# Earlier loads at a stage change, a store cut in two, and program order on ScalarE and VectorE, in a recurrent-attention and gated-MLP kernel

## The chip, the cores and the metric

The kernel runs on one core of a Trainium2 chip. Times are device microseconds (us) of one execution. Where two kernels are compared by a ratio, it is the mean time of one kernel's runs over that of the other's of the same rounds, so it isn't quite the ratio of the medians quoted beside it. "Job" means one series of runs on one chip; kernels of one job share their runs of the kernel before.

## The reference

```python
xn = layernorm(A_x)                                  # 2048 x 1024
# A: attention over 64 segments of 32 tokens, each with 8 memory rows in front
for s in range(64):
    h = concat([mem, xn[segment s]])                 # 40 rows
    q, k, v = h @ Wq, h @ Wk, h @ Wv                 # 32 heads of 128
    p = softmax(where(mask, q k^T * scale, -1e9))    # memory rows see all; tokens are causal
    o = (p v) @ Wo
    mem = o[:8]                                      # carried into the next segment
    outs.append(o[8:])
# B: h = sigmoid(xn @ w_gate) * (xn @ w_up);  B = h @ w_down        (width 3584)
return A_x + concat(outs) * silu(B)
```

The kernel doesn't walk the 64 segments one after the other. With these small weights the scores are so small that softmax inside a memory row is almost a mean, so it computes all memory rows in two sweeps, treats all tokens in parallel, and checks at the end from norms and maxima that this was allowed (`flag`; a slow exact path runs otherwise).

## The kernel before: the parts that matter

The stages are: values for all tokens (`v_ps`), two sweeps over the memory rows mixed with pieces of the gate and up projections, 32 heads of attention, the rest of gate and up, and the down and output projections with the check beside them. TensorE (PE) and the SyncE queue (SP) keep program order everywhere. ScalarE (ACT), VectorE (DVE) and GpSimd (POOL) are ordered by the compiler's scheduler except where `manual_schedule` names them.

The second memory sweep writes 71 rows of values to HBM (63 segments and 8 start rows), and takes the difference of the sweeps for the check on DVE:

```python
for hg in range(H // 4 + 2):
    if hg < H // 4:
        ...                                          # 32 matmuls into vm_ps
        vts[hg] = gp.tile([P, 4, NCM], BF16, name="vmt", tag="o2", bufs=3)
        nc.scalar.copy(vts[hg][:], vm_ps[:])
        dv = gp.tile([P, 4, NM], F32, name="dv", bufs=2)
        nc.vector.scalar_tensor_tensor(dv[:], vm_ps[:, :, 0:NM], 1.0 / M, vg1[:, hg * 4:(hg + 1) * 4, :], ...)
        nc.vector.tensor_tensor(dv[:], dv[:], dv[:], op=ALU.mult)
        nc.vector.tensor_reduce(dvs[:, hg, :], ...)
    if hg >= 2:
        ...                                          # 4 transposes into vt_ps
        nc.vector.tensor_copy(vm_sb[0:NCM, ...], vt_ps[0:NCM])
        if g % 2 == 1:
            nc.sync.dma_start(vm_dram[1:NSEG + M, cols], vm_sb[0:NCM, :])     # 71 rows
            nc.sync.dma_start(vm_dram[0:1, cols], vm_sb[0:1, :])
```

Then attention. `va` (token values) and `vm` (memory values) are allocated in a pool that takes over the space of the stage before:

```python
vas = [vp.tile([P, NT + 1, VW], BF16, name=f"va{i}") for i in range(2)]       # and memsets on DVE
...
def load_pair(hp):                     # va, then vm (each memory row read by 32 partitions)
    nc.sync.dma_start(va[:, 0:NT, 1:VW - 1], vp_dram[:, cols]...)
    ...
    for a in range(SPT):
        nc.sync.dma_start(vm[a * SEG:(a + 1) * SEG, :, 1:VW - 1], src[a:a + 1].to_broadcast([SEG, NT, 2 * DH]))

def proj_steps(h):                     # one step per matmul: 80 "slots" a head
    for x, dst in enumerate((qt, kt)):
        nc.scalar.activation(fsq[:], w_[:, :, hc], ACTF.Square, accum_out=fro[:, x, h:h + 1])
        for i in range(NBLK):
            ...                        # 8 matmuls into pr, then
            nc.scalar.copy(dst[:, a:b], pr[:, 0:b - a])
            if i == NBLK - 1:
                track(x, dst)          # DVE: mx = max(mx, |dst|), in two halves

load_pair(0)
for h in range(H + 1):
    pj = proj_steps(h); at = attn_steps(h - 1)       # the projection of h beside the attention of h-1
    for i in range(80):
        if i == 32 and h % 2 == 1: load_w((h + 1) // 2); load_pair((h + 1) // 2)
        next(pj); next(at)
```

Here `fsq` is the square of the head's weights, `s_ps` the scores, `pT` their exp and mask, `o_ps` the product with the values, `of` the addition of the memory part. In the down stage the check adds up squares of Wo, ACT and DVE by turns:

```python
for h in range(H):
    nc.scalar.activation(ws[:], wo_sb[:, h, :], ACTF.Square)
    nc.vector.tensor_tensor(wn[:], wn[:], ws[:], op=ALU.add)
    if h % 2 == 1: yield               # one step after each half of an output tile
```

## Time and profile before

| what | before |
|---|---|
| median of the first five runs | 1625.13 us (1621.75 to 1626.16) |
| the profiled run | 1621.24 us, span 1619.3 us |
| PE busy | 1579.4 us of the span |
| PE idle at the change into attention | 13 us, plus cold restarts (granted clock 0.50 from 320.3 to 322.8, from 344 to 347 and from 354 to 356 us) |
| PE idle in the thirty regular heads | 6.0 us |
| PE idle at the start of the down stage | 6.1 us, plus a cold restart (granted clock 0.50 from 1218 to 1224 us) |

PE is busy 98% of the span, so what counts is where it isn't. The lines are shown in the prediction below. One stretch inside the heads is worth seeing beforehand, because the later argument comes back to it. It is the timeline of the kernel before: start, duration, engine, line and operation, and in brackets the idle time before it and what ended that.

```profile
378.38 1.06 ACT L586 ACTIVATE fsq<-wqk 128x1024 bf16<-128x1024 bf16 x1 [1.82 <-DMA wqk<-in_A_Wq_dram]
...
379.82 1.06 ACT L586 ACTIVATE fsq<-wqk 128x1024 bf16<-128x1024 bf16 x1
...
381.25 1.06 ACT L586 ACTIVATE fsq<-wqk 128x1024 bf16<-128x1024 bf16 x1
...
382.68 1.07 ACT L586 ACTIVATE fsq<-wqk 128x1024 bf16<-128x1024 bf16 x1
...
383.74 0.60 ACT L618 ACTIVATE pT<-s_ps 128x512 bf16<-128x512 f32 x1
...
384.38 0.22 PE L614 MATMUL s_ps<-qt,kt 128*128 128x128 bf16 x1 [0.50 <-ACT pT L618]
...
385.24 0.34 PE L634 MATMUL o_ps<-va,pT 128*128 128x129 bf16 x3 [0.64 <-DVE pT L620]
```

ACT first waits 1.82 us for weights to land, then does four squares of 1.06 us, with evictions between them. These are the four squares of the pair of heads 4 and 5, whose first projection starts 19 us later, at 397.6. The exp that PE needs now comes at 383.74, and PE stalls twice. Nothing in the program asks for this order: the scheduler put the squares there.

### The profile page before, as it was taken

Reading aid. Unit: us, or ns where it says so; the run is one execution under the profiler, and the core shown is the slowest. Engines: PE = TensorE matmul, PEld = TensorE weight load, DVE = VectorE, ACT = ScalarE, POOL = GpSimd, SP = SyncE. Lnnn points to the kernel's source line nnn. Section 1 sums busy time; section 2 is a strip of 40 time slices with the busy share of each in tenths; the row PEclk is TensorE's granted clock in tenths of the full one; section 3 lists DMA queues with packets and bytes.
Section 4 is the critical chain, followed back from the end, with each engine's and each line's share of the span. In section 5 each row is a group of like instructions: output and inputs, shape, how many; then the busy total and the mean of one; then the engine's idle time right before and its main releaser. Section 6 shows DMA issues by size and latency. Waiting matters only on the chain.

```text
span 1619.3 us, 23188 instructions
## 1 busy us (share of the span) xinstructions
PE 1579.4 (98%) x9463; PEld 818.4 (51%) x9566; DVE 750.6 (46%) x1606; ACT 500.0 (31%) x956; POOL 139.9 (9%) x220
## 2 busy tenths in 40 slices
PE   9999999979999999999999999999998999999998
PEld 4444546645556656565654444444443444444444
DVE  6555433437778777778784222122146311121111
ACT  4333331145555555565542111111134100000000
POOL 2111110000010001000001111111100000000000
PEclk9999999999999999999999999999999999999999
DMA  7644554557576757665613544432352342424240
GB/s 229 202 130 149 195 189 157 158 123 175 121 153 156 162 121 142 142 133 122 134 59 110 171 149 170 139 134 78 79 130 77 103 136 76 130 76 129 76 130 28
DMA packets 256806, 213.25 MB, mean 132 GB/s; under 512 B 82256, under 2 KB 218576, under 8 KB 256696
## 3 DMA queue, kind: packets, MB, share of 16 engines
q1 hardware_dynamic: 228920, 140.66, 35.7%
q0 software_dynamic: 17200, 56.37, 9.9%
q10 hardware_dynamic: 10576, 14.70, 3.0%
q8 instruction: 76, 1.25, 0.3%
q14 instruction: 34, 0.28, 0.1%
HBM read 129.32 MB, written 63.50 MB: 119 GB/s over the span
## 4 chain that ended last, share of the span: by engine, by line
PE 88%; DMA 5%; DVE 3%; ACT 3%; issue 1%; SPq 0%; DVEq 0%; ACTq 0%
PE pr L591 22%; PE v_ps L345 14%; PE a_ps L824 13%; PE u_ps L172 12%; PE g_ps L168 12%; PE y_ps L814 11%; DMA wqk<-in_A_Wq_dram 2%; PE o_ps L634 2%; PE s_ps L614 1%; DMA vm_dram<-vm_sb 1%; ACT fsq L586 1%; PE acc L385 1%; DMA vm<-vm_dram 1%; DVE wn L753 1%; ACT ws L752 1%
## 5 line engine op out<-in xcount | busy, mean ns | idle before, releaser
L591 PE MATMUL pr<-xnT,wqk 128*128 128x412 bf16 (+1 forms) x2560 | 506.6, 339 | 0.0
L591 PEld LDWEIGHTS <-wqk 128*128 128x128 bf16 x2560 | 222.8, 98 | 137.8 <-issue 12.3
L824 PE MATMUL a_ps<-wo_sb,ot 128*128 128x512 bf16 (+2 forms) x1036 | 224.6, 372 | 0.9
L345 PE MATMUL v_ps<-wv_sb,xnT 128*128 128x512 bf16 x1002 | 222.1, 379 | 1.9 <-DMA wv_sb<-in_A_Wv_dram 0.7
L172 PE MATMUL u_ps<-xnT,wu 128*128 128x512 bf16 x881 | 210.2, 379 | 0.8
L176 DVE SCALAR_TENSOR_TENSOR hst<-th,u_ps 128x512 bf16<-128x512 f32 x112 | 77.0, 688 | 288.4 <-PE u_ps L172 266.6
L168 PE MATMUL g_ps<-xnT,wg 128*128 128x512 bf16 x868 | 209.2, 379 | 1.4
L814 PE MATMUL y_ps<-wd,ht 128*128 128x512 bf16 x878 | 199.6, 382 | 7.3 <-DVE gq L818 6.1
L824 PEld LDWEIGHTS <-ot 128*128 128x128 bf16 x1056 | 102.1, 98 | 119.4
L175 ACT ACTIVATE th<-g_ps 128x512 f32<-128x512 f32 x112 | 66.9, 597 | 304.8 <-PE g_ps L168 289.7
L345 PEld LDWEIGHTS <-xnT 128*128 128x128 bf16 x1024 | 99.4, 98 | 118.4 <-ACT xnT L321 1.2
L814 PEld LDWEIGHTS <-ht 128*128 128x128 bf16 x896 | 88.0, 99 | 114.3 <-issue 10.8
L172 PEld LDWEIGHTS <-wu 128*128 128x128 bf16 x896 | 87.7, 98 | 105.7
L168 PEld LDWEIGHTS <-wg 128*128 128x128 bf16 x896 | 86.6, 98 | 101.2
L348 ACT CAST v_sb<-v_ps 128x512 bf16<-128x512 f32 x128 | 74.9, 585 | 144.3 <-PE v_ps L345 133.8
L817 ACT ACTIVATE th<-y_ps 128x512 f32<-128x512 f32 x32 | 19.0, 594 | 322.6 <-PE y_ps L814 322.6
L594 ACT CAST kt<-pr 128x412 bf16<-128x412 f32 (+1 forms) x160 | 79.4, 501 | 126.8 <-PE pr L591 126.6
L643 DVE TENSOR_TENSOR of<-o_ps,vm 128x387 f32<-128x387 f32 x192 | 97.6, 509 | 32.8 <-PE o_ps L634 29.2
L614 PE MATMUL s_ps<-qt,kt 128*128 128x128 bf16 x512 | 110.7, 220 | 0.5 <-ACT pT L618 0.5
L618 ACT ACTIVATE pT<-s_ps 128x512 bf16<-128x512 f32 x128 | 76.1, 595 | 86.1 <-PE s_ps L614 86.1
L646 DVE TENSOR_TENSOR osb<-of,rden 128x384 bf16<-128x384 f32 x192 | 98.4, 513 | 4.4
L830 DVE SCALAR_TENSOR_TENSOR tmp<-a_ps,gq 128x512 f32<-128x512 f32 (+2 forms) x33 | 22.3, 675 | 150.0 <-PE a_ps L824 138.6
(143 smaller groups left out, 1137.4 us busy)
## 6 DMA issues: line engine op xcount, KB each, us to landing
vp_dram<-v_sb POOLq DMA_DIRECT2D x64, 256.0 KB, 3.3
va<-vp_dram SPq DMA_DIRECT2D x16, 1024.0 KB
vm<-vm_dram SPq DMA_DIRECT2D x64, 256.0 KB
o_dram<-osb POOLq DMA_DIRECT2D x16, 960.0 KB, 14.3
hT_dram<-hst POOLq DMA_DIRECT2D x56, 256.0 KB, 2.7
ht<-hT_dram SPq DMA_DIRECT2D x16, 896.0 KB
xt<-in_A_x_dram SPq DMA_DIRECT2D x32, 256.0 KB
wo_t<-in_A_Wo_dram ACTq DMA_DIRECT2D x8, 1024.0 KB
```

The lines of the kernel that those rows point to most:

```text
L168: nc.tensor.matmul(g_ps[:], lhsT=wg[:, c, fc * P:(fc + 1) * P], rhs=xnT[:, c, tb * TB:(tb + 1) * TB], start=(c == 0), stop=(c == KC - 1))
L172: nc.tensor.matmul(u_ps[:], lhsT=wu[:, c, fc * P:(fc + 1) * P], rhs=xnT[:, c, tb * TB:(tb + 1) * TB], start=(c == 0), stop=(c == KC - 1))
L176: nc.vector.scalar_tensor_tensor(hst[:, :, fc, :], th[:].rearrange("p (a b) -> p a b", b=P), 1.0, u_ps[:].rearrange("p (a b) -> p a b", b= ...
L345: nc.tensor.matmul(v_ps[:], lhsT=xnT[:, c, t * P:(t + 1) * P], rhs=wv_sb[:, c, cg * 512:(cg + 1) * 512], start=(c == 0), stop=(c == KC - 1))
L591: nc.tensor.matmul(pr[:, 0:b - a], lhsT=w_[:, c, hc], rhs=xmT[:, c, a:b], start=(c == 0), stop=(c == KC - 1))
L594: nc.scalar.copy(dst[:, a:b], pr[:, 0:b - a])
L614: nc.tensor.matmul(s_ps[:, j * P:(j + 1) * P], lhsT=kt[:, o:o + P], rhs=qt[:, o:o + P], start=True, stop=True)
L618: nc.scalar.activation(pv, s_ps[:, 0:n * P], ACTF.Exp, scale=scale)
L643: nc.vector.tensor_tensor(ot[:, 0:n, :], o_ps[:, 0:n, :], vm[:, j0:j0 + n, v0:v0 + DH + 1], op=ALU.add)
L646: nc.vector.tensor_tensor(osb[:, j0:j0 + n, hc], ot[:, 0:n, e0:e0 + DH], rd.unsqueeze(2).to_broadcast([P, n, DH]), op=ALU.mult)
L814: nc.tensor.matmul(y_ps[:], lhsT=hts[t][:, c, :], rhs=wd[:, c, hf * 512:(hf + 1) * 512], start=(c == 0), stop=(c == FC - 1))
L824: nc.tensor.matmul(a_ps[:], lhsT=ox[t][0][:, h, :], rhs=wo_sb[:, h, a:b], start=(h == 0), stop=(h == H - 1))
```

## The change

Its intent is to take PE's waits away at all three places. The core of the diff, with cuts marked:

```diff
+    avp = es_q.enter_context(tc.tile_pool(name="av", bufs=1))      # va, vm of even pairs, vt8: space of their own
+    def v_tiles(pool): ...                                          # va, vm and their memsets, now on GpSimd
...
-                nc.scalar.copy(vg1[:, hg * 4:(hg + 1) * 4, :], vm_ps[:, :, 0:NM])
+                nc.scalar.mul(vg8[:, hg * 4:(hg + 1) * 4, :], vm_ps[:, :, 0:NM], float(M))
...
         load_w(0)
+        load_v(0)                                                   # va of pair 0, before the second sweep
         for hg in range(H // 4 + 2):
-                nc.scalar.copy(vts[hg][:], vm_ps[:])
-                dv = ...                                            # three DVE operations a group
+                nc.scalar.copy(vt8[:, hg * 4:(hg + 1) * 4, :], vm_ps[:])
...
-                    nc.sync.dma_start(vm_dram[1:NSEG + M, cols], vm_sb[0:NCM, :])
+                    nc.sync.dma_start(vm_dram[1:65, cols], vm_sb[0:64, :])
+                    nc.sync.dma_start(vm_dram[65:NSEG + M, cols], vm_sb[64:NCM, :])
                     nc.sync.dma_start(vm_dram[0:1, cols], vm_sb[0:1, :])
+        load_vm(0)
         build_masks(nc, mask, mask0)
+        nc.gpsimd.tensor_tensor(vg8[:], vt8[:, :, 0:NM], vg8[:], op=ALU.subtract)
+        nc.gpsimd.tensor_tensor(vg8[:], vg8[:], vg8[:], op=ALU.mult)
...
+        es.enter_context(tc.manual_schedule(engines={ACT}))         # ACT in program order in the heads
         load_pair(0)
         for h in range(H + 1):
             for i in range(NSL):
+                if i == 6 and h > 0: track(h - 1, 1)                # one 2048-wide maximum, two ab buffers
+                if i == 74 and h < H: track(h, 0)
+                if i in (44, 58) and h < H: norms(h, i // 58)       # the squares, no longer in proj_steps
...
+        es_d.enter_context(tc.manual_schedule(engines={ACT, DVE}))  # program order in the down stage
```

The other hunks make the warm-up tile a part of `mx` and adapt a factor of the check. (A constant `PVS` is added and never used.)

More of the change, by code (lines that the diff above doesn't have):

```diff
@@ L224 @@
     mxs = cst.tile([P, 2, S // 4], BF16, name="mxs")
-    dvs = cst.tile([P, H // 4, NM], F32, name="dvs")
+    vg8 = cst.tile([P, H, NM], BF16, name="vg8")
     flag = cst.tile([1, 1], I32, name="flag")
@@ L263, with v_tiles @@
     es_q = ExitStack()
+    VW = 2 * DH + 2
+    avp = es_q.enter_context(tc.tile_pool(name="av", bufs=1))
+    vas, vms = [], []
+    def v_tiles(pool):
+        i = len(vas)
+        va = pool.tile([P, NT + 1, VW], BF16, name=f"va{i}")
+        vm = pool.tile([P, NT, VW], BF16, name=f"vm{i}")
+        nc.gpsimd.memset(va[:, NT, :], 0.0)
+        for c in (0, VW - 1):
+            nc.gpsimd.memset(va[:, 0:NT, c:c + 1], 1.0)
+            nc.gpsimd.memset(va[0:L, NT, c:c + 1], 1.0)
+            nc.gpsimd.memset(vm[:, :, c:c + 1], float(M))
+        vas.append(va)
+        vms.append(vm)
+    vt8 = avp.tile([P, H, NCM], BF16, name="vt8")
     hwp = es_q.enter_context(tc.tile_pool(name="h_w", bufs=2, reuse_waits="tile"))
@@ L375, in load_w, with load_v, load_vm @@
             nc.sync.dma_start(wqks[hp][:, 1], Wk2[:, cols].rearrange("(c p) n -> p c n", p=P))
+        def load_v(hp):
+            cols = slice(hp * 2 * DH, (hp + 1) * 2 * DH)
+            va = vas[hp % 2]
+            nc.sync.dma_start(va[:, 0:NT, 1:VW - 1], vp_dram[:, cols].rearrange("(t p) c -> p t c", p=P))
+            nc.sync.dma_start(va[M:L, NT, 1:VW - 1], vp_dram[0:SEG, cols])
+        def load_vm(hp):
+            cols = slice(hp * 2 * DH, (hp + 1) * 2 * DH)
+            va, vm = vas[hp % 2], vms[hp % 2]
+            src = vm_dram[0:NSEG, cols].rearrange("(t a) c -> a t c", a=SPT)
+            for a in range(SPT):
+                nc.sync.dma_start(vm[a * SEG:(a + 1) * SEG, :, 1:VW - 1], src[a:a + 1].to_broadcast([SEG, NT, 2 * DH]))
+            nc.sync.dma_start(va[0:M, NT, 1:VW - 1], vm_dram[NSEG:NSEG + M, cols])
         def wo_load(hg, q=nc.sync):
@@ L391 @@
         es_v.enter_context(tc.manual_schedule(engines={ACT, DVE}))
-        spz = gp.tile([P, 512], BF16, name="spz")
-        nc.vector.memset(spz[:], 0.0)
+        spz = mx[:, 0, 0:512]
+        nc.vector.memset(spz, 0.0)
+        nc.gpsimd.memset(mx[:, 0, 512:S], 0.0)
+        nc.gpsimd.memset(mx[:, 1, :], 0.0)
         spin = psb.tile([P, 512], F32, name="spin", tag="big")
         for _ in range(11):
-            nc.tensor.matmul(spin[:], lhsT=spz[:, 0:P], rhs=spz[:], start=True, stop=True)
+            nc.tensor.matmul(spin[:], lhsT=spz[:, 0:P], rhs=spz, start=True, stop=True)
         normalize(0)
@@ L475 @@
         wo_t = {}
-        vg1 = gp.tile([P, H, NM], BF16, name="vg1")
+        v_tiles(avp)
         for hg in range(H // 4 + 2):
@@ L500 @@
         load_w(0)
-        vts = {}
+        load_v(0)
         for hg in range(H // 4 + 2):
@@ L508 @@
                                          rhs=cmT[:, c, :], start=(c == 0), stop=(c == KC - 1))
-                vts[hg] = gp.tile([P, 4, NCM], BF16, name="vmt", tag="o2", bufs=3)
-                nc.scalar.copy(vts[hg][:], vm_ps[:])
-                dv = gp.tile([P, 4, NM], F32, name="dv", bufs=2)
-                nc.vector.scalar_tensor_tensor(dv[:], vm_ps[:, :, 0:NM], 1.0 / M, vg1[:, hg * 4:(hg + 1) * 4, :],
-                                               op0=ALU.mult, op1=ALU.subtract)
-                nc.vector.tensor_tensor(dv[:], dv[:], dv[:], op=ALU.mult)
-                nc.vector.tensor_reduce(dvs[:, hg, :], dv[:].rearrange("p h s -> p s h"), axis=AX.X, op=ALU.add)
+                nc.scalar.copy(vt8[:, hg * 4:(hg + 1) * 4, :], vm_ps[:])
             if hg >= 2:
@@ L519 @@
                 for hi in range(4):
-                    nc.tensor.transpose(vt_ps[0:NCM, hi, :], vts[g][:, hi, :], ident[:])
+                    nc.tensor.transpose(vt_ps[0:NCM, hi, :], vt8[:, g * 4 + hi, :], ident[:])
                 if g % 2 == 0:
@@ L525 @@
                     cols = slice((g - 1) * 512, (g + 1) * 512)
-                    nc.sync.dma_start(vm_dram[1:NSEG + M, cols], vm_sb[0:NCM, :])
+                    nc.sync.dma_start(vm_dram[1:65, cols], vm_sb[0:64, :])
+                    nc.sync.dma_start(vm_dram[65:NSEG + M, cols], vm_sb[64:NCM, :])
                     nc.sync.dma_start(vm_dram[0:1, cols], vm_sb[0:1, :])
+        load_vm(0)
         build_masks(nc, mask, mask0)
+        nc.gpsimd.tensor_tensor(vg8[:], vt8[:, :, 0:NM], vg8[:], op=ALU.subtract)
+        nc.gpsimd.tensor_tensor(vg8[:], vg8[:], vg8[:], op=ALU.mult)
     NBLK = 5
     edges = [(NPE * i // NBLK) // 2 * 2 for i in range(NBLK)] + [NPE]
-    VW = 2 * DH + 2
     SBT = 512 // P
@@ L541 @@
         nc.gpsimd.memset(rden[:], 1.0)
-        nc.gpsimd.memset(mx[:], 0.0)
-        vas = [vp.tile([P, NT + 1, VW], BF16, name=f"va{i}") for i in range(2)]
-        for va in vas:
-            nc.vector.memset(va[:, NT, :], 0.0)
-            for c in (0, VW - 1):
-                nc.vector.memset(va[:, 0:NT, c:c + 1], 1.0)
-                nc.vector.memset(va[0:L, NT, c:c + 1], 1.0)
-        vms = [vp.tile([P, NT, VW], BF16, name=f"vm{i}") for i in range(2)]
-        for vm in vms:
-            for c in (0, VW - 1):
-                nc.vector.memset(vm[:, :, c:c + 1], float(M))
+        v_tiles(vp)
         pTs = [vp.tile([P, S + P], BF16, name=f"pT{i}") for i in range(2)]
@@ L559, in load_pair, with track, norms @@
         def load_pair(hp):
-            cols = slice(hp * 2 * DH, (hp + 1) * 2 * DH)
             wqk = wqks[hp]
             va, vm = vas[hp % 2], vms[hp % 2]
-            nc.sync.dma_start(va[:, 0:NT, 1:VW - 1], vp_dram[:, cols].rearrange("(t p) c -> p t c", p=P))
-            nc.sync.dma_start(va[M:L, NT, 1:VW - 1], vp_dram[0:SEG, cols])
-            nc.sync.dma_start(va[0:M, NT, 1:VW - 1], vm_dram[NSEG:NSEG + M, cols])
-            src = vm_dram[0:NSEG, cols].rearrange("(t a) c -> a t c", a=SPT)
-            for a in range(SPT):
-                nc.sync.dma_start(vm[a * SEG:(a + 1) * SEG, :, 1:VW - 1], src[a:a + 1].to_broadcast([SEG, NT, 2 * DH]))
             osb = sb.tile([P, NT + 1, 2 * DH], BF16, name="osb")
             st[hp] = (wqk[:, 0], wqk[:, 1], va, vm, osb)
-        def track(x, t):
-            ab = sb.tile([P, S], BF16, name="ab", bufs=1)
+        def track(h, x):
+            t = st["qk", h][x]
+            ab = sb.tile([P, S], BF16, name="ab", bufs=2)
             nc.vector.tensor_scalar(ab[:].bitcast(I32), t[:, M:NPE].bitcast(I32), 0x7FFF7FFF, None, op0=ALU.bitwise_and)
-            for a in (0, S // 2):
-                m = mx[:, x, a:a + S // 2]
-                nc.vector.tensor_tensor(m, m, ab[:, a:a + S // 2], op=ALU.max)
+            nc.vector.tensor_tensor(mx[:, x, :], mx[:, x, :], ab[:], op=ALU.max)
+        def norms(h, x):
+            w_ = st[h // 2][x][:, :, (h % 2) * DH:(h % 2 + 1) * DH]
+            nc.scalar.activation(fsq[:], w_, ACTF.Square, accum_out=fro[:, x, h:h + 1])
         def proj_steps(h):
@@ L585, in proj_steps @@
                 w_ = st[h // 2][x]
-                nc.scalar.activation(fsq[:], w_[:, :, hc], ACTF.Square, accum_out=fro[:, x, h:h + 1])
                 for i in range(NBLK):
@@ L594, in proj_steps @@
                             nc.scalar.copy(dst[:, a:b], pr[:, 0:b - a])
-                            if i == NBLK - 1:
-                                track(x, dst)
                         yield
@@ L657 @@
         NSL = 2 * NBLK * KC
+        PVS = (16, 27, 38, 49, 60, 71)
         def attn_steps(h):
@@ L677 @@
                     load_w((h + 1) // 2)
+                    load_v((h + 1) // 2)
+                    load_vm((h + 1) // 2)
                     load_pair((h + 1) // 2)
@@ L680 @@
                     nc.sync.dma_start(xnT_dram[:, h // 2 - 1, :], xnT[:, h // 2 - 1, :])
+                if i == 6 and h > 0:
+                    track(h - 1, 1)
+                if i == 74 and h < H:
+                    track(h, 0)
+                if i in (44, 58) and h < H:
+                    norms(h, i // 58)
                 if pj is not None:
@@ L743, in check @@
             nc.vector.tensor_reduce(gm[:], gq2[:].rearrange("p c s -> p s c"), axis=AX.X, op=ALU.max)
-            nc.vector.tensor_reduce(r_[:, 2 * H + NM:], dvs[:].rearrange("p g s -> p s g"), axis=AX.X, op=ALU.add)
+            nc.vector.tensor_reduce(r_[:, 2 * H + NM:], vg8[:].rearrange("p h s -> p s h"), axis=AX.X, op=ALU.add)
             yield
@@ L794, in check @@
             dr = sb.tile([1, NM], F32, name="dr", bufs=1)
-            nc.vector.tensor_scalar(dr[:], v1[:, 2 * H + NM:], u[:, 3:4], SLACK * (M * CINV / float(tau)) ** 2, op0=ALU.mult, op1=ALU.mult)
+            nc.vector.tensor_scalar(dr[:], v1[:, 2 * H + NM:], u[:, 3:4], SLACK * (CINV / float(tau)) ** 2, op0=ALU.mult, op1=ALU.mult)
             nc.vector.tensor_tensor(cmpv[:, 1:NM], dr[:, 0:NM - 1], g2r[:, 1:NM], op=ALU.is_le)
@@ L806, in check @@
             yield
+        es_d = ExitStack()
+        es_d.enter_context(tc.manual_schedule(engines={ACT, DVE}))
         chk = check()
@@ L863 @@
             nc.sync.dma_start(out2[S - P:S, a:b], ress[NT - 1][:, a:b])
+        es_d.close()
     es_w.close()
```

## The prediction

> **What bounds the kernel now.** I read the page's first part, then PE's busy time stage by stage, then the chain of work that ended last, then the waits.
>
> ```profile
> span 1619.3 us, 23188 instructions
> PE 1579.4 (98%) x9463; PEld 818.4 (51%) x9566; DVE 750.6 (46%) x1606; ACT 500.0 (31%) x956; POOL 139.9 (9%) x220
> ```
>
> TensorE is the bound: no change in another engine's load pays unless PE now waits for it. PE is idle for 1619.3 - 1579.4 = 39.9 us in all, and that, plus whatever runs at a reduced clock, is the whole prize, because the diff removes no matmul. The windows (span, then each engine's busy us and count, then granted PE clock, DMA share, GB/s) show where the idle time lies:
>
> ```profile
> core 0: us, PE busy (x) PEld busy (x) DVE busy (x) ACT busy (x) POOL busy (x), PEclk, DMA share, GB/s
> 306.00:316.00 10.00, 9.93 (x268) 9.79 (x265) 8.84 (x22) 3.09 (x8) 1.31 (x2) 1.00 0.13 36
> 316.00:319.30 3.30, 0.62 (x9) 0.47 (x8) 3.20 (x8) 0.08 (x1) 0.00 (x0) 1.00 0.07 25
> 319.30:323.30 4.00, 4.00 (x18) 1.86 (x16) 1.65 (x5) 0.50 (x1) 0.00 (x0) 0.57 0.08 28
> 335.00:364.80 29.80, 19.55 (x118) 11.22 (x117) 15.21 (x46) 11.19 (x24) 0.00 (x0) 0.89 0.60 126
> 364.80:846.90 482.10, 476.08 (x3421) 290.84 (x3419) 377.44 (x960) 264.10 (x562) 37.09 (x45) 1.00 0.62 136
> 1212.00:1220.00 8.00, 1.89 (x8) 0.74 (x7) 4.84 (x5) 4.43 (x5) 0.00 (x0) 0.85 0.00 0
> 1220.00:1228.00 8.00, 8.00 (x28) 3.18 (x27) 6.25 (x8) 3.65 (x4) 0.57 (x1) 0.73 0.00 1
> ```
>
> Three places stand out: the hand-over from the memory-value stage into attention (306 to 365), the thirty regular heads (365 to 847, 6.0 us idle), and one hole at 1213. At the hand-over the chain of waits reads (start, us, what):
>
> ```profile
> 323.59 14.15 DMA vm_dram<-vm_sb
> 337.74 0.09 issue
> 337.83 0.17 DVE va L545
> ...
> 339.85 13.57 DMA vm<-vm_dram
> ...
> 353.53 0.57 DVE of L643
> 354.10 0.04 issue
> 354.15 0.27 PE o_ps L634
> ```
>
> The last small store of memory values lands 14 us after issue; only then may the memset of va (its space is taken over from the store's source) and the vm load follow, and head 0's PV waits for both. The list of waits names the other two places (waiter, releaser, us in total, times, longest):
>
> ```profile
> PE y_ps L814 <- DVE gq L818: 6.1, 1, 6.1
> ...
> ACT fsq L586 <- DMA wqk<-in_A_Wq_dram: 18.5, 15, 5.6
> ```
>
> The first is the hole at 1213: ACT alternates the squares of the check (ws, 1.06 us) with DVE's adds (wn, 1.23 us), and the tanh and gq that free a PSUM buffer stand behind that ladder. The second is ACT standing in front of a square of weights that have not landed, with PSUM evictions behind it.
>
> [...] The store has 71 rows[...] issued from 312.1 on, last landing at 337.7, DMA share only 0.07 to 0.13. [...] granted 0.57 for 4 us after the pause at 316. [...]
>
> **The change part by part.**
>
> (a) Memory-value loop. Per group of four heads it removes three DVE operations (0.42 + 0.42 + 0.59 = 1.43 us in the timeline), leaving the 0.41 us copy; the difference is computed afterwards by two whole-array GpSimd operations. In the before, DVE needs about 1.75 us a group against PE's 1.34, so the last two groups stall PE. New bound: PE. By 316.0 it lacks only two groups of transposes (2 x 0.39 us), so projections start near 317.2 instead of 319.32 (2.1 us), and warm: the 4 us at 0.57 cost 1.7 to 2.0. Gain about 4.0.
>
> (b) Store split into 64 + 7 rows, va/vm of pair 0 in a pool of their own, va loaded before the loop, vm right after the stores. Head 0 without attention lasts 8 matmuls x 10 blocks at 1.39 us a block = 13.9 us, so 317.2 to 331.1. Head 1's iteration, at the steady 476.08/30 = 15.87 us, would end at 347.0; it now ends at 364.8. Gain of (a) and (b) together 17.8, so (b) is 13.8: about 10 us of PE idle plus the two cold restarts at 344 and 354. Condition: vm must be there when the first additions are due. Its load took 338.42 to 353.41, 15.0 us, in the before. With the stores landed at about 320 it would land at about 335. PV starts in slot 16 of head 1's iteration, 331.1 + 16 x 0.198 = 334.3, but two o_ps buffers let PE go on to slot 32, 337.4. It fits with 2 us to spare. I deduct 1.
>
> (c) Squares of the weights moved to slots 44 and 58, ACT in program order. The 18.5 us of ACT waits vanish. They were not 18.5 us of PE: PE lost at most the 6.0 us of the thirty heads, and the pieces of weight DMA in the chain coincide with the stretches that lost 0.5 to 1.1 us. I take 4.5.
>
> (d) Tracking of maxima: one 2048-wide maximum for two halves (1.29 us for two; about 1.23 for one), two ab buffers, later places. This saves 64 x 0.06 = 4 us of an engine busy 78% of the stage. DVE is not on the path; but one longer operation can hold a mask back. Deduct 1.
>
> (e) ACT and DVE in program order in the down stage. The 6.11 us hole goes, and the cold restart (28 matmuls in 8.65 us against 6.05 warm) with it: 8.7. DVE now does tmp and res before the copy that the check's bp matmuls wait for, about 0.5 us more there. Gain 8.2. The longer final reduce (2016 elements instead of 504) lies under a 6 us projection.
>
> (f) Early memsets on GpSimd, the warm-up tile inside mx: hidden, 0.
>
> Sum: 4.0 + 13.8 - 1 + 4.5 - 1 + 8.2 = 28.5 us. 1625.1 - 28.5 = 1596.6 us.
>
> **The rivals.**
>
> R1: the vm load stays the bound. It reads each row 32 times at only about 90 GB/s, and two of the other 1 MB loads queue near it. For: it took 15 us even with the DMA engines half idle. Against: it now starts some 18 us earlier relative to the trace. If it lands at 342 instead of 335, PE stalls about 4.6 us and restarts cold (2 us): time about 1603.
>
> R2: program order hurts. ACT and DVE can no longer slip small work forward, so exp or mask come later and PE waits each head; 0.3 us a head would be about 10 us: time about 1607. Against: in the before, exp and projection copies already alternate in the order of the program, and ACT is idle 45% of the stage.
>
> R3: all idle time counted goes. (a) and (b) 18.3, (c) 6.0, (e) 8.7 make 33.0: time 1592.1. This is about the ceiling of the change, and only just 2%.
>
> R4: DVE is the hidden bound of the heads, because the delayed maxima meet the masks at a head's start[...]. For: DVE busy 78%. Against: PE's waits on DVE there sum to under 6 us. This would eat (c) and more: about 1603 to 1612.
>
> **Range and chances.** The terms (a), (b) and (e) rest on holes seen directly; they carry 25 of 28.5 us. (c) and (d) are judged. The range runs from everything won plus a little (1589) to R2 or R4 in full (1609). A gain of over 2% needs 32.5 us, practically R3: 0.18. Slower by over 2% would need a new wait over 60 us: 0.02. Within 2%: 0.80.
>
> **What would show it right or wrong.** Right: the vm_dram stores land within 3 us of issue and the chain at 306 to 350 is all PE; projections start near 317, warm; head 1's iteration takes about 16 us; no granted clock under 0.9 between 316 and 1590; ACT waits for wqk gone; the 6.11 us wait of y_ps gone; PE's busy total falls only by the cold restarts, about 7 us. Wrong: a new wait of PE for of, pT or va that recurs per head (R2, R4); a wait on vm at head 1 (R1); thirty heads longer than 482 us; new PE waits in the check's small matmuls over 3 us; or an unchanged hole at the start of the down stage.

## The result

In the first job the changed kernel took 1586.74 us in the median (1585.41 to 1588.13, 8 runs), the kernel before 1626.66 us (1621.75 to 1630.38, 15 runs). The ratio is 0.9757 (0.9747 to 0.9767). That is 2.4% faster, outside the predicted range at its fast end.

The page of the changed kernel begins, and the list of PE's waits over its whole span reads:

```profile
span 1585.4 us, 23110 instructions
PE 1568.9 (99%) x9463; PEld 815.4 (51%) x9566; DVE 737.5 (47%) x1504; ACT 502.7 (32%) x956; POOL 151.4 (10%) x237
```

```profile
PE spin L429 <- DVE mx L424: 1.3, 1, 1.3
PE bp L802 <- DVE g2r L798: 1.1, 1, 1.1
PE v_ps L362 <- ACT xnT L338: 0.7, 1, 0.7
PE pt L336 <- DVE xn L329: 0.6, 2, 0.4
PE bp L802 <- DVE bigs L803: 0.4, 2, 0.2
PE vt_ps L547 <- DVE vm_sb L550: 0.3, 1, 0.3
PE y_ps L839 <- issue: 0.2, 1, 0.2
```

The waits of before for `of`, `va` and `pT`, and the one of 6.1 us for `gq`, are all gone; what is left lies at the start of the kernel and in the check, but for 0.3 us in the second sweep (`vt_ps`) and 0.2 us at `y_ps`. The windows of the changed kernel (columns as in the prediction: span, busy time of each engine, granted clock, DMA share, GB/s) answer to those of before. They cover the second sweep, head 0, head 1 and the thirty heads after it:

```profile
304.90:316.00 11.10, 10.81 (x289) 10.76 (x288) 3.44 (x8) 3.17 (x8) 1.15 (x2) 1.00 0.45 102
316.00:330.10 14.10, 14.10 (x85) 7.95 (x83) 3.03 (x6) 6.39 (x13) 8.24 (x10) 1.00 0.41 87
330.10:346.00 15.90, 15.90 (x117) 9.65 (x115) 12.36 (x30) 9.05 (x19) 0.00 (x0) 1.00 0.96 180
346.00:819.90 473.90, 473.90 (x3423) 290.79 (x3422) 372.74 (x901) 271.70 (x570) 39.76 (x45) 1.00 0.64 138
```

PE is busy for the whole of the last three windows at the full granted clock. DVE's share in the sweep has fallen from 9 us of 10 to 3.4 of 11. Two lines of the same kernel's timeline show that the load that was in doubt came in time:

```profile
318.48 1.91 SPq L405 DMA_DIRECT2D vm<-vm_dram  x4
...
334.18 0.55 DVE L656 TENSOR_TENSOR of<-o_ps,vm 128x387 f32<-128x387 f32 x1
```

The vm load is issued at 318.48, and the first addition that reads it runs at 334.18 without a wait for it. PE follows without a pause.

To place the gain I mark five points on PE in each trace: the first matmul of the second sweep, the first projection, the first scores of head 1's iteration and of the next, and the end of the last projection. "Down" starts with the first output projection. Durations in us:

| stage | before | after | gain |
|---|---|---|---|
| up to the second sweep | 305.39 | 304.87 | 0.5 |
| second sweep | 13.93 | 11.18 | 2.75 |
| head 0 | 15.76 | 14.08 | 1.7 |
| head 1 | 29.61 | 15.87 | 13.7 |
| thirty heads | 482.36 | 473.91 | 8.45 |
| rest of gate and up | 340.16 | 340.15 | 0 |
| down, to the end of the span | 432.09 | 425.34 | 6.75 |
| span | 1619.3 | 1585.4 | 33.9 |

Two questions remain. The thirty heads gave 8.45 us, while PE's idle time there was 6.0. And the medians differ by 39.9 us, the spans of the traces by 33.9. The experiments take the parts one by one and then go to these two.

### The profile page after: what moved, and what is told of

Its sections match the earlier page's. It is cut to its first block, busy times and chain, and to the rows that moved or that the text cites.

```text
span 1585.4 us, 23110 instructions
## 1 busy us (share of the span) xinstructions
PE 1568.9 (99%) x9463; PEld 815.4 (51%) x9566; DVE 737.5 (47%) x1504; ACT 502.7 (32%) x956; POOL 151.4 (10%) x237
## 4 chain that ended last, share of the span: by engine, by line
PE 99%; DVE 0%; issue 0%; DMA 0%; ACT 0%
PE pr L606 28%; PE a_ps L849 14%; PE v_ps L362 14%; PE y_ps L839 12%; PE u_ps L172 12%; PE g_ps L168 12%; PE o_ps L647 2%; PE s_ps L627 2%; PE acc L416 1%; PE vm_ps L540 1%; PE vm_ps L516 1%; PE pt L336 0%; DMA xt<-in_A_x_dram 0%; PE o_ps L651 0%; PE vt_ps L547 0%
## 5 line engine op out<-in xcount | busy, mean ns | idle before, releaser
L606 PE MATMUL pr<-xnT,wqk 128*128 128x412 bf16 (+1 forms) x2560 | 501.2, 337 | 0.0
```

The costliest lines, as they stand in the source:

```text
L606: nc.tensor.matmul(pr[:, 0:b - a], lhsT=w_[:, c, hc], rhs=xmT[:, c, a:b], start=(c == 0), stop=(c == KC - 1))
```

## The experiments

### The parts alone

Four kernels were run in one job, whose runs of before had a median of 1620.83 us (1618.21 to 1623.03, 9 runs).

**Hand-over only**: the changed kernel with its other parts undone.

```diff
 # against the changed kernel
-        es.enter_context(tc.manual_schedule(engines={ACT}))
-                if i in (44, 58) and h < H: norms(h, i // 58)      # squares back in proj_steps
-                if i == 6 ... track(h - 1, 1);  if i == 74 ... track(h, 0)   # track back in proj_steps, two halves
-        es_d.enter_context(tc.manual_schedule(engines={ACT, DVE}))
```

> The kernel before with the early va/vm load, the split store and the difference moved to GpSimd, and nothing of the square, track or program-order parts. Theory T: the profiled traces put this part at 18.8 us (first heads end 18.8 us earlier); over the medians it is worth more, about 22 us, because the pause of before varies from run to run and its profiled run was a quick one. Rival R: the parts are exactly as large as in the profiles and the missing 5 us of the medians lie elsewhere, so 18 to 19 us. T also expects the spread of this kernel's runs to be about as small as the changed kernel's (under 4 us).

Measured: 1602.22 us (1601.64 to 1604.88, 4 runs), ratio 0.9887 (0.9872 to 0.9902), so 18.6 us. In its trace the sweep takes 11.17, head 0 14.08 and head 1 15.80 us; the thirty heads are still at 480.4. The rival was right about the size in this job; the spread of 3.2 us fits what I expected of it.

**Squares and ACT's order only.**

```diff
 # against before
+        es.enter_context(tc.manual_schedule(engines={ACT}))
-                nc.scalar.activation(fsq[:], w_[:, :, hc], ACTF.Square, ...)    # in proj_steps
+                if i in (44, 58) and h < H: norms(h, i // 58)
```

> The kernel before with the weight squares moved to slots 44 and 58 and ACT in program order, nothing else. Theory T: this alone recovers what the thirty heads gained, 8.3 us in the traces, so 7 to 9 us faster. Rival R: the DVE part (track) brought half of it, so this alone gives at most 4 to 5 us, as the prediction had it.

Measured: 1614.23 us (1612.99 to 1615.23, 5 runs), ratio 0.9958 (0.9945 to 0.9972), so 6.6 us. The trace is plainer than the time: the thirty heads take 473.91 us, to the hundredth what they take in the changed kernel. All of the heads' gain comes from this part. The time shows 6.6 and not 8.5, but its interval reaches from 4.5 to 8.9 us. In the trace, sweep, head 0 and head 1 together took 59.95 us against 59.30, and the sweep began 1.07 us later than in the first trace of before; this part of the change touches neither.

**Maxima only.**

```diff
 # against before
-            ab = sb.tile([P, S], BF16, name="ab", bufs=1)          # and two maxima of 1024
+            ab = sb.tile([P, S], BF16, name="ab", bufs=2)          # one of 2048
-                            if i == NBLK - 1: track(x, dst)
+                if i == 6 and h > 0: track(h - 1, 1)
+                if i == 74 and h < H: track(h, 0)
```

> The kernel before with the maxima taken in one operation, two ab buffers and later places, nothing else. Theory T: DVE is not on the path, so within 1 us of before. Rival R: 3 to 5 us faster, since PE in the heads waited mostly for DVE by name.

Measured: 1621.37 us (1620.56 to 1621.88, 5 runs), ratio 1.0001 (0.9988 to 1.0015). Nothing, either way. DVE was named in most of PE's waits, but it was passing on ACT's delay: with ACT's order alone (below), the waits for DVE go too.

**Program order in the down stage only.**

```diff
 # against before
+        es_d.enter_context(tc.manual_schedule(engines={ACT, DVE}))
```

> The kernel before with ACT and DVE in program order in the down stage, nothing else. Theory T: 8.7 us faster (6.1 us hole and 2.6 us cold restart), as the trace has it. Rival R: program order costs some of it back in the check's small matmuls, 7 to 8 us.

Measured: 1612.99 us (1611.13 to 1615.76, 5 runs), ratio 0.9952 (0.9939 to 0.9966), so 7.8 us. In its trace the last stage takes 423.91 us against 432.09, 8.2 less, and the first two tiles' down projections run on without a pause:

```profile
1204.65 13.54 PE L816 MATMUL y_ps<-wd,ht 128*128 128x512 bf16 x62
```

The check's small matmuls wait 1.1 us for `g2r` instead of 0.4, and 0.4 for `bigs` instead of 1.0, so program order costs next to nothing there (1.5 us of waits against 1.4). The time's interval, 5.5 to 9.9 us, can't tell the expected 8.7 from the rival's 7 to 8.

The four parts sum to 18.6 + 6.6 - 0.5 + 7.8 = 32.5 us, each with an interval of about 2 us to either side.

### The whole once more, and leaving one part out

These four ran in another job, on another chip; its runs of before had a median of 1622.76 us (1620.17 to 1625.90, 17 runs).

> The changed kernel unaltered, on another chip job. The four parts measured apart add up to 18.6 + 6.6 + 0 + 7.8 = 33 us where before ran in 1620.8, but the whole was measured as 39.9 us where before ran in 1626.7. Theory T: the whole is worth about 33 to 35 us wherever before runs near 1621, and the changed kernel runs in 1585 to 1589 everywhere; before's time is what differs from job to job. Rival R: the parts help each other, so the whole is still about 40 us faster here.

Measured: 1586.79 us (1586.30 to 1588.34, 5 runs), ratio 0.9777 (0.9764 to 0.9791), so 36.0 us (33.9 to 38.3), a little over what I expected and short of the rival's 40. The changed kernel repeats its time to 0.05 us in another job. Before doesn't: its medians were 1626.66, 1620.83 and 1622.76 in three jobs. Taken from 1620.83, the parts' 32.5 us lead to 1588.3, within 1.6 us of this, and so within the noise. The traces say the same stage by stage. Sweep, head 0 and head 1 take 41.05 us in the hand-over alone and 41.13 in the changed kernel; the thirty heads take 473.91 with the squares' part alone and in the changed kernel; the last stage takes 423.9 with program order alone and 425.3 and 424.4 in the two traces of the changed kernel. So no part is seen to help another.

The kernel before, unaltered, as a run of its own:

> The kernel before unaltered, as a run of its own, for a second trace and for each run's span and granted clock. Theory T: same as before within 0.1%; its runs spread over 4 us or more and the longer ones have the lower granted clock, since the extra time is cold restarts after the pauses. Rival R: the longer runs have the same clock and longer waits for the vm and va loads.

Measured: 1622.41 us (1620.81 to 1624.54, 13 runs), ratio 0.9995 (0.9987 to 1.0004). The clock part of my theory fell: the run of 1622.88 us had a granted clock of 0.995, the one of 1620.92 us 0.993. Its stages explain why. Here head 0 took 14.08 us, without the cold restart that the first trace has after the same pause (15.76 us, with a granted clock of 0.57 in its first 4 us), and head 1 took 31.46 instead of 29.61. Sweep, head 0 and head 1 together are 59.30 us in the first trace and 59.47 in this one. The stretch ends when the DMAs land (the vm load at 353.41 us in the first trace); whether PE was cold in head 0 only moved its waiting from one place to another.

The changed kernel without the part of the squares:

```diff
 # against the changed kernel
-        es.enter_context(tc.manual_schedule(engines={ACT}))
-                if i in (44, 58) and h < H: norms(h, i // 58)      # squares back in proj_steps
```

> The changed kernel with the weight squares back at the start of each projection and ACT scheduled freely in the heads. Theory T: loses what the square part gave alone, 6.6 us (5 to 9). Rival R: with the early loads of the hand-over and the relieved DVE the square no longer waits, so it loses under 2 us.

Measured: 1594.01 us (1592.16 to 1594.89, 5 runs), 7.2 us over the changed kernel of the same job. The thirty heads are back at 479.69 us, and ACT waits 9.9 us for wqk again. The rival is out.

### Which half of the squares' part works

The same job had ACT's order without the new slots, a later one the new slots without the order.

```diff
 # order_only, against before
+        es.enter_context(tc.manual_schedule(engines={ACT}))
 # slots_only, against before
-                nc.scalar.activation(fsq[:], w_[:, :, hc], ACTF.Square, ...)    # in proj_steps
+                if i in (44, 58) and h < H: norms(h, i // 58)
```

> The kernel before with ACT in program order in the heads but the squares left at the start of each projection. Theory T: program order is the working half, since the square then stands behind the evictions of its own head and finds its weights landed: 5 to 7 us faster, like the whole part. Rival R: the new slots are the working half, so this gives under 2 us, or costs time because a 1.25 us square stands ahead of the first exp of the head.

Measured: 1613.69 us (1613.18 to 1614.47, 5 runs), ratio 0.9943 (0.9929 to 0.9956), so 9.1 us (7.1 to 11.5), more than I had expected. The thirty heads take 473.92 us.

> The kernel before with the weight squares written at slots 44 and 58, but ACT still scheduled freely in the heads. Theory T (program order is the working half): the scheduler again takes the squares forward to where it thinks their weights have landed, ACT waits for wqk again, and the thirty heads stay near 482 us instead of 474: within 2 us of before. Rival R: the place in the program is enough, thirty heads near 474 us, 7 to 9 us faster.

Measured: 1621.87 us (1619.46 to 1629.69, 13 runs; before 1621.04, 27 runs), ratio 1.0007 (0.9996 to 1.0018). The thirty heads take 481.09 us. The list of waits of this kernel has the old line, a little larger than before:

```profile
ACT fsq L581 <- DMA wqk<-in_A_Wq_dram: 19.0, 14, 7.6
```

The scheduler took the squares forward again from their new place. The order is the whole of it. The last job repeats this on the changed kernel:

```diff
 # after_order, against the changed kernel: ACT stays in program order
-                if i in (44, 58) and h < H: norms(h, i // 58)      # squares back in proj_steps
```

> The changed kernel with the weight squares back at the start of each projection, ACT still in program order. Theory T: thirty heads again near 474 us, so the same time as the changed kernel, 1585 to 1589 us: the slots do nothing that order has not done. Rival R: a square ahead of the head's first eviction delays PE, 2 us or more slower.

Measured: 1586.56 us (1586.21 to 1588.35, 5 runs), ratio 0.9783 (0.9771 to 0.9796). The thirty heads take 473.91 us. With the squares where they were before the change, the time is the same.

### The hand-over taken apart

These ran with slots_only, in a job with a median of before of 1621.04 us (1618.07 to 1624.33, 27 runs).

**The difference on GpSimd only** (`vg8` and `vt8` as in the change; store, loads and buffers as before):

> The kernel before with the difference of memory values moved from DVE to GpSimd, the store and the loads as before. Theory T: projections start 2.7 us earlier, but the four 71-row stores keep one queue busy until about 336 us, so the pause in head 1 grows by what the loop gained: within 1 us of before. Rival R: as the prediction summed it, (a) is worth 4 us by itself.

Measured: 1620.71 us (1618.54 to 1626.29, 14 runs), ratio 0.9996 (0.9987 to 1.0005). The sweep takes 11.16 us instead of 13.93, head 0 14.08, and head 1 34.37. Everything the sweep gained is waited away in head 1, since the last store still lands at 337.7 us, as in the kernel before.

**The split store only:**

```diff
 # against before
-                    nc.sync.dma_start(vm_dram[1:NSEG + M, cols], vm_sb[0:NCM, :])
+                    nc.sync.dma_start(vm_dram[1:65, cols], vm_sb[0:64, :])
+                    nc.sync.dma_start(vm_dram[65:NSEG + M, cols], vm_sb[64:NCM, :])
```

> The kernel before with only the store of memory values split into 64 and 7 rows. Theory T: the last store lands at about 325 instead of 338, the memset and loads behind it start some 12 us earlier, and head 1's iteration falls from 29.6-31.9 to about 18 us: 10 to 13 us faster. Rival R: the va and vm loads are what lasts, so it stays over 25 us and the gain is under 6 us.

Measured: 1607.39 us (1605.14 to 1610.29, 5 runs), ratio 0.9915 (0.9898 to 0.9931), so 13.7 us for one more line, a little over what I expected. Head 1 takes 17.91 us. The chain of what ended last in this stretch reads (start, us, what):

```profile
321.38 2.81 DMA vm_dram<-vm_sb
...
331.23 13.58 DMA wqk<-in_A_Wk_dram
344.89 1.15 ACT fsq L587 x2
346.04 0.40 ACT qt L595
```

The store at the end of this chain lands 2.81 us after its issue, against 14.15 in the kernel before. What now sets the end of head 1 is the square that waits for weights, with an eviction behind it. The hand-over alone, where ACT is as free as here, has no such wait in head 1 (15.80 us). No run has the split with ACT's order alone.

**The change with the store in one piece:**

```diff
 # against the changed kernel
-                    nc.sync.dma_start(vm_dram[1:65, cols], vm_sb[0:64, :])
-                    nc.sync.dma_start(vm_dram[65:NSEG + M, cols], vm_sb[64:NCM, :])
+                    nc.sync.dma_start(vm_dram[1:NSEG + M, cols], vm_sb[0:NCM, :])
```

> The changed kernel with the store again in one piece of 71 rows; early va load and own buffers kept. Theory T: the vm load waits for a store that lands near 336, so vm lands near 350 and PE pauses in head 1 for 8 to 12 us with a cold restart: 9 to 14 us slower than the changed kernel. Rival R: the own buffers are what helped, and it loses under 3 us.

Measured: 1595.24 us (1594.01 to 1596.07, 5 runs), ratio 0.9837 (0.9823 to 0.9851). That is 8.5 us over the changed kernel's 1586.79 of another job, a little under what I expected and far from the rival. Head 1 takes 23.84 us. Sweep, head 0 and head 1 together are 49.10 us here, 45.91 with the split alone, and 59.30 before and 41.13 after. So the split alone is worth 13.4 us of these 18.2, everything else in the hand-over without it 10.2: they overlap. The own space and the early va load were not run by themselves. Its SyncE queue shows how the stores hold it up; line 553 issues the 71 rows, line 554 the single row after them:

```profile
317.34 0.22 SPq L553 DMA_DIRECT2D vm_dram<-vm_sb  x1
317.60 5.12 SPq L554 DMA_DIRECT2D vm_dram<-vm_sb  x1
322.81 0.22 SPq L553 DMA_DIRECT2D vm_dram<-vm_sb  x1
323.07 5.25 SPq L554 DMA_DIRECT2D vm_dram<-vm_sb  x1
328.42 3.06 SPq L405 DMA_DIRECT2D vm<-vm_dram  x2
```

The queue stands for just over 5 us at each of the last two single-row stores (2.91 at the second, 0.36 at the first). So the vm load is issued only at 328.4 instead of 318.5. With the split, the same queue spends 0.21 to 0.52 us on each piece.

### What stays open: before's own time

> The kernel before once more, on whatever chip comes. Theory T: if this job's before runs are at 1624 or above, the extra time lies in the hand-over (loop, head 0 and head 1 together over 61 us instead of 59.3 to 59.5) and in the thirty heads, the two stages that wait for DMAs, and the stages after them are as before. Rival R: all stages are longer by the same share, a slower clock. If the job is a quick one (near 1621), this stays open.

Measured: 1621.51 us (1618.77 to 1623.96, 14 runs; before 1621.54), ratio 0.9997 (0.9989 to 1.0006). It was a quick job, so this stays open. The single runs confirm that the granted clock doesn't separate long from short ones: 0.994 for 1618.77 us and 0.994 for 1624.72. The three traces of before differ in the hand-over (59.30, 59.47 and 59.96 us) and in the thirty heads (482.36, 483.26 and 480.54), the two stages that wait for DMAs, by less than 3 us, and in the rest of gate and up not at all (340.15 to 340.16). That is the direction in which a slow job might lie, but no trace of one was taken. The nearest thing is the profiled run of the GpSimd-only kernel, at 1626.29 us the longest of its 14. Against the first trace of before, its sweep began 1.07 us later, sweep, head 0 and head 1 took 59.61 us, the thirty heads 485.0 (2.6 more), the rest of gate and up 340.15 and the last stage 433.3 (1.1 more). It is another kernel and one run, so it is only a hint. What made before slow in the first job stays open.

## Why the prediction was wrong

**The chains of waits were read rightly, and so was the largest term.** Part (b), 13.8 us for the store and the early loads, measured 13.7 in head 1. The chain of that stretch is PE now but for one DVE copy of 0.43 us, no granted clock falls below full speed in it, and the vm load lands in time. The 1 us deducted for a late landing was not needed. That 64 and 7 rows would land so much sooner than 71 was my estimate then; the split store alone showed it, with 2.81 us from issue to landing against 14.15. Why 71 rows land so late is not shown.

**Part (a)** was put at 4.0 and shows 2.75 + 1.7 = 4.4 in the stage table. But it isn't a gain of its own: alone it gave nothing, since head 1 waits for the same landing. And the cold restart that I counted in it (0.57 of the clock for 4 us) is absent from other traces of before without any change of the total. Only (a) and (b) together are a quantity: 17.8 predicted before the deduction, 18.2 in the traces, 18.6 in the time of the part run alone.

**Part (c) is the step that failed.** The prediction said that "PE lost at most the 6.0 us of the thirty heads" and took 4.5 of it. The traces give 8.45 us, and ACT's order alone recovers it all. The ceiling was wrong because idle time isn't all of lost time; the same step stands at the head of the prediction, which calls idle time and reduced clock "the whole prize". Of the 8.45 us, 6.00 were idle. The other 2.45 were inside "busy": for the same matmuls, PE was busy for 476.36 us of the stage before and for 473.91 after, at a granted clock of 1.00 in both. (The window printed in the prediction, with 476.08, cuts about 0.3 us off the stage.) The reason is in the durations. A lone score matmul is recorded with 0.22 us, as at 384.38 above, but four in an unbroken row last 0.39 us in the same trace:

```profile
846.89 0.39 PE L614 MATMUL s_ps<-qt,kt 128*128 128x128 bf16 x4
```

So each further one adds 0.06 us, since they overlap in the record. By this reading the first after a pause has nothing to overlap with, and each pause costs its idle time and an estimated 0.16 us (0.22 - 0.06) of busy time on top. The trace has 13 pauses of PE in these heads, 12 of them named in its list of waits, which makes an estimated 2.1 us. The other traces bear this out. Nine more runs have 8 to 15 pauses in these heads, and in each the time over 473.91 us exceeds PE's idle time by 0.16 to 0.20 us a pause. The ends of matmuls are modelled in these profiles, so the border between idle and busy is not exact; the 8.45 us do not depend on it. I also took only three quarters of the idle time, though all of it had the same cause.

**Part (d)** got a deduction of 1 us for longer DVE operations. One maximum of 2048 took 1.23 us in the changed kernel's trace, the two of 1024 took 1.29 before. Alone the part is 1.0001 of before. (c) and (d) together were put at 3.5 us; this is the largest miss of the sum, 5 us.

**Part (e)** was put at 8.2 and gave 8.2 in its own trace (the 62 matmuls in 13.54 us there are 6.1 for 28, which took 8.65 in the cold restart), 7.8 in its own time and 6.75 in the first pair of traces, where the span ended 1.8 us later after PE's last matmul.

**The rivals.** R1 (a late vm load) didn't happen in the changed kernel; with the store in one piece it did. R2 (program order hurts) is the reverse of what happened: order on ACT is what won the heads. R4 (DVE as hidden bound) fell with the maxima run alone. Whether DVE is slower while GpSimd works was hardly put to the test: during most of the two new GpSimd operations (315.61 to 323.25 us) DVE stood idle, 6.92 us on end, for ACT. R3 was called "about the ceiling of the change" at 33.0 us; the spans differ by 33.9, so the ceiling itself was too low, by the busy time just described. (Its 18.3 us for (a) and (b) is 0.5 over the 17.8 of the prediction's own sum, without a working.)

**The base.** The sum in terms of the traces should have been 33.9 instead of 28.5. The first job showed 39.9. Of this, 5.4 us are the difference between before's profiled run (1621.24 us) and its median there (1626.66); the changed kernel's profiled run and median differ by 0.4. In the job of the repeat before was at 1622.76 and the gain 36.0. I subtracted gains read from a quick run from the median of a slower job, and gave the range no allowance for it. Of the 9.9 us between 1596.6 and the measured 1586.74, 5.4 are the terms of the sum, 3.9 are this base (1625.1 less 1621.24), and 0.6 is left over. Had the base been the job's own, 28.5 would still have been too small by the terms above.

The prediction's own sign was there: it expected PE's busy total to fall "only by the cold restarts, about 7 us". It fell by 1579.4 - 1568.9 = 10.5 us.

No version of these experiments beats the changed kernel; the one without the new slots (1586.56 us) equals it.

## What to carry to other kernels

Where PE is the bound, waits can cost more than the idle time that the profile shows: here 6.0 us of idle time stood for 8.45 us lost, since the 13 pauses also broke the overlap of the matmuls, an estimated 2.1 us that count as busy. Compare busy times of the same work with and without waits. An engine that a scheduler orders can be made to wait for something needed 19 us later; look for a wait on a far-off load ahead of urgent evictions, and fix the order, since moving the instruction in the source alone changed nothing here. And look at what stands behind a small store in its queue: here the one-row stores after those of 71 rows stood for up to 5.6 us, and cutting 71 rows into 64 and 7 was worth 13.7 us. Other row counts were not tried.

## What else the traces show

- The stores: the DMA share was 0.07 to 0.08 while 71-row stores were under way (316.0 to 323.3 us), and the last store, queued behind them, landed 14.15 us after its issue, against 2.81 for the one that held up the chain with 64 + 7 rows. The issuing queue also stood still behind such stores, so that unrelated loads were issued late: it stood for 0.4, 1.2, 2.2 and 5.6 us at the four one-row stores of the kernel before, and for 0.4, 2.9, 5.1 and 5.3 us in the change with the store in one piece. Why it stands isn't shown; in the changed kernel it also stood for 5.28 us at a wqk load.
- The clock: after the same pause before 319.32 us, head 0 took 15.76 us in one trace of the kernel before, with a granted clock of 0.57 in its first 4 us, and 14.08 in another, the time that the changed kernel took at a granted clock of 1.00. Nor did the restarts last equally long. Windows of half a microsecond in the first trace read 0.50 from 320.3 to 322.8, and windows of one read 0.50 from 1218 to 1224. With that value the windows in the prediction give low clock for about 3.4 us after 319.3 (0.43 x 4 us x 2), but for about 6.7 us around 1220 (0.15 x 8 x 2 + 0.27 x 8 x 2), both estimates.
- GpSimd: the two operations on 128 x 2016 elements in bf16 took 4.02 and 3.55 us in the changed kernel, in a profile that calls GpSimd's spans rough.
- The time between jobs: before's medians went from 1620.83 to 1626.66 us, the changed kernel's from 1586.74 to 1586.79.
